# Attention with a mixture of soft experts: another opening, a reordered step between the two, and one weight piece issued sooner

## The chip, the cores and the metric

The kernel runs on one core of a Trainium2 chip. The metric is the device time of one execution in microseconds (us). TensorE (PE) multiplies matrices, VectorE (DVE) and ScalarE (ACT) work on vectors, GpSimd (POOL) fills buffers here, and SyncE (SP) issues all transfers between the chip's main memory and the core's buffers. Each engine runs its instructions in the order in which the program gives them; engines wait for each other through semaphores.

## What is computed

The reference has two stages. The first is attention in chunks: 4 batches, 8 heads, 768 positions, 64 values a head. Each chunk of 32 queries sees 8 memory keys and 56 keys around it.

```python
for c in range(nc):
    k_full = np.concatenate([mem_k, k_ctx], axis=2)
    v_full = np.concatenate([mem_v, v_ctx], axis=2)
    scores = scale * np.matmul(q_c, k_full.transpose(0, 1, 3, 2))
    a = np.exp(scores - np.max(scores, axis=-1, keepdims=True))
    a = a / (np.sum(a, axis=-1, keepdims=True) + 1e-09)
    out[:, :, c_start:c_end] = np.matmul(a, v_full)
```

Its result, as 3072 rows x of 512, goes into the second stage. Each of 32 slots takes a weighted mean of all rows (a softmax over the rows), eight experts of two layers work on four slots each, and every row takes a weighted mean of the slots' results (a softmax over the slots).

```python
logits = x @ phi
d = softmax(logits, over rows); slot_input = d.T @ x
for e in range(E):
    h = np.maximum(slot_input[e] @ w1[e], 0.0)
    slot_out[e] = h @ w2[e]
c = softmax(logits, over slots); out = c @ slot_out
```

All numbers are 32-bit floats. The two layers of weights are a bit over half of what the kernel reads.

## The kernel before, in words

**Units.** Attention goes over 24 tiles of 128 queries, two to a unit: units n = 0 to 11 (the loop in line 354). For a unit, `load_q`, `load_k` and `load_v` bring queries, keys and value rows into one of two slabs each (`kq_slab`, `v_slab`; unit n uses slab n % 2). Even and odd partitions of a slab hold the two heads of a pair; a transfer of keys or values fills one parity and one half, and the rest of the slab has to be zero. That zeroing is done once, in the opening (lines 150 to 161): VectorE and GpSimd share slab 0 of the keys and both slabs of the values, ScalarE does both halves of slab 1 of the keys, by copying zeros. Twelve dummy matmuls (`keep_warm(12)`) keep TensorE occupied until the keys are there.

**One unit on TensorE.** Transposes of the probabilities (`pt_ps`), the scores of the next unit (`s`), in every second unit the logits of the group before (`l`) or the dispatch of one (`D_ps`), transposes of the finished rows (`xt_ps`), and the values (`a`). VectorE does maxima, subtractions, sums and normalizing, ScalarE the exponentials and copies out of PSUM.

**Groups.** Four tiles of rows are a group G; there are six. For each, `logits` multiplies with phi, `dispatch_max` keeps a running maximum (`nmx`, in the tile `stats`) and copies the logits (`lT`), `dispatch_exp` takes the exponential, `dispatch_t` transposes it, `dispatch` multiplies it with the rows (`D_ps`), and `dispatch_sum` adds that to the running sum `D_sb`.

**The step between attention and experts** (lines 400 to 461). Groups 4 and 5 (NG - 2 and NG - 1) are still open here. TensorE transposes the last rows, dispatches group 4, takes the logits of group 5, brings the maximum of each slot to all partitions (`nmb`, `nm_ps`, `nms`, `b_ps`, `wrow`, `selw`), dispatches group 5, and makes the slots' input (`si_ps`, copied to `siT`), with which the experts begin (`h`). The normalizer of the slots (`wz`, `z_ps`, `rzd`) is made behind that. Groups of dummies stand between these.

**Experts and the end.** `expert_in` runs the first layer in four pairs of experts, `expert_out` the second layer, in two halves of the columns (`so`), and `combine` multiplies the combine weights with the slots' results and stores them (`o`).

**Weights and the transfer queue.** All transfers are issued by SyncE in program order, so one that waits holds back those behind it. The weights come in 32 pieces of 1 MB: 16 of w1, 16 of w2. Twelve slabs (`w_slab`, w_70 to w_81 in the order of instructions below) are theirs alone; eight more are the slabs of keys, values and rows once attention is done with them. `load_w(upto)` issues pieces up to a number: unit n asks for n + 2 pieces (line 398), from unit 9 on for as many as have a slab (`usable`). At unit n SyncE issues query and keys of unit n + 3, then value rows of unit n + 2, then that piece. A transfer also waits until the one eight places ahead of it in the queue has landed, because eight semaphores are used in turn.

```python
        if n + 2 < NUNIT:
            load_v(n + 2)
        load_w(usable[n] if n >= NUNIT - 3 else n + 2)
```

Of the kernel before, what the change touches and what calls it, by code (L numbers as in the profile page):

```python
# [10 lines left out]
F32 = mybir.dt.float32  # L11
F32R = mybir.dt.float32r
AF = mybir.ActivationFunctionType
ALU = mybir.AluOpType
AX = mybir.AxisListType

P = 128
# [7 lines left out]
NU = B * UPB  # L25
UU = 2
NUNIT = NU // UU
# [3 lines left out]
KB = NPAIR * KW  # L31
# [35 lines left out]
def tile_attn_softmoe(  # L67
# [44 lines left out]
    def load_v(n):  # L112
        t = v_slab[n % NIN]
        for par in range(2):
            sp.dma_start(t[par:P:2, par], vw[n, par])
# [28 lines left out]
    def keep_warm(n):  # L144
        if n:
            w_ps = ps.tile([P, P], F32, tag="T", name="fill_ps", bufs=2)
            for _ in range(n):
                pe.matmul(w_ps, lhsT=warm, rhs=warm, start=True, stop=True)

    dve.memset(warm, 0.0)  # L150
    dve.memset(kq_slab[0][:, 0:KB], 0.0)
    pool.memset(kq_slab[0][:, KB:2 * KB], 0.0)
    make_identity(nc, ident)
    for i in range(NIN):
        dve.memset(v_slab[i][:, 0], 0.0)
        pool.memset(v_slab[i][:, 1], 0.0)
    for par in range(2):
        act.copy(
            out=kq_slab[1][:, KB * par:KB * par + KB].rearrange("p (o n) -> p o n", n=104),
            in_=warm[:, 0:104].rearrange("p (o n) -> p o n", o=1).broadcast_to([P, KB // 104, 104]),  # L160
        )
    keep_warm(12)

    load_q(0)
    load_q(1)
# [1 line left out]
    load_k(1)  # L167
    load_v(0)
    sp.dma_start(phi_sb, phi.rearrange("(kc p) s -> p kc s", p=P))
    dve.tensor_reduce(out=sel, in_=ident.rearrange("p (g s) -> p s g", s=NSLOT), axis=AX.X, op=ALU.add)  # L170
    pool.tensor_copy(out=gsum, in_=sel.rearrange("p (o s) -> p o s", o=1).broadcast_to([P, 4, NSLOT]))

# [99 lines left out]
    def dispatch_max(G, l_ps):  # L272
        dve.tensor_reduce(out=nmx[G], in_=l_ps, axis=AX.X, op=ALU.max, negate=True)
        if G:
            dve.tensor_tensor(out=nmx[G], in0=nmx[G], in1=nmx[G - 1], op=ALU.min)
        lT[G] = wk.tile([P, P], F32, tag="lT", name=f"lT{G}")
        dve.tensor_copy(out=lT[G], in_=l_ps)

    def dispatch_exp(G, l_ps):
        d = wk.tile([P, P], F32, tag="d", name=f"d{G}", bufs=1)  # L280
        act.activation(out=d, in_=l_ps, func=AF.Exp, bias=nmx[G], scale=1.0, accum_out=zg[G])
        dexp[G] = d
        if G:
            act.activation(out=alpha[G], in_=nmx[G - 1], func=AF.Exp, bias=nmx[G], scale=-1.0)
# [32 lines left out]
        pe.transpose(t_ps, c[G].rearrange("p u s -> p (u s)"), ident)  # L317
        act.copy(out=cst[:, G, :], in_=t_ps)

    def dispatch(G):  # L320
        D_ps = ps.tile([P, DM], F32, tag="L", name=f"D_ps{G}")
        for g in range(4):
            pe.matmul(
                D_ps[32 * g:32 * g + 32, :],
                lhsT=dT[G][:, 32 * g:32 * g + 32],
                rhs=x_slab[G % 2][:, g, :],
                start=True, stop=True,
            )
        return D_ps

    def dispatch_z(G):
        if G:
            dve.scalar_tensor_tensor(out=zg[G], in0=zg[G - 1], scalar=alpha[G], in1=zg[G], op0=ALU.mult, op1=ALU.add)
# [14 lines left out]
    for u in range(UU):  # L348
        softmax(u, scores(u))
    load_kq(2)  # L350
    load_v(1)
    load_w(1)
    a_ps = {}
    for n in range(NUNIT):
        us = (2 * n, 2 * n + 1)
        last = n + 1 == NUNIT
        Gl = (n - 3) // 2 if n >= 3 and n % 2 == 1 else None
        Gd = (n - 4) // 2 if n >= 4 and n % 2 == 0 else None
        pts = [transpose_p(u) for u in us]
        if n >= 1:  # L360
            for u in us:
                normalize(u - 2, a_ps[u - 2])
        normalizer(n)
        if not last:
            s_ps = [scores(u + 2) for u in us]
        if n + 3 < NUNIT:
            load_kq(n + 3)
        if Gd is not None:
            dispatch_t(Gd)
        if Gl is not None:  # L370
            l_ps = logits(Gl)
        if n >= 1:
            transpose_x(us[0] - 2)
        if not last:
            for u, t in zip(us, s_ps):
                softmax(u + 2, t)
        if Gd is not None:
            combine_exp(Gd)
        if Gl is not None:
            dispatch_max(Gl, l_ps)  # L380
            dispatch_exp(Gl, l_ps)
            if Gl >= 1:
                combine_div(Gl - 1)
        a_ps[us[0]] = values(us[0], pts[0])
        if last:
            transpose_x(us[1] - 2)
            normalize(us[0], a_ps[us[0]])
            dispatch_t(NG - 2)
        a_ps[us[1]] = values(us[1], pts[1])
        if n >= 1 and not last:  # L390
            transpose_x(us[1] - 2)
        if Gd is not None:
            D_ps = dispatch(Gd)
            dispatch_z(Gd)
            dispatch_sum(Gd, D_ps)
        if n + 2 < NUNIT:
            load_v(n + 2)
        load_w(usable[n] if n >= NUNIT - 3 else n + 2)

    normalize(NU - 1, a_ps[NU - 1])  # L400
    transpose_x(NU - 2)
    D_ps = dispatch(NG - 2)
    load_w(usable[NUNIT])
    keep_warm(1)
    dispatch_z(NG - 2)
    dispatch_sum(NG - 2, D_ps)
    transpose_x(NU - 1, last=True)
    keep_warm(3)
    l_ps = logits(NG - 1)
    combine_in(NG - 2)  # L410
    dispatch_max(NG - 1, l_ps)
    dispatch_exp(NG - 1, l_ps)
    keep_warm(4)

    nm = nmx[NG - 1]
    nm_ps = ps.tile([NSLOT, 4, NSLOT], F32, tag="X", name="nm_ps")
    nmb = wk.tile([P, NSLOT], F32, tag="nmb", name="nmb", bufs=1)
    dve.tensor_copy(out=nmb, in_=nm.broadcast_to([P, NSLOT]))
    pe.transpose(nm_ps.rearrange("p g s -> p (g s)"), nmb, ident)
    nms = wk.tile([NSLOT, NSLOT], F32, tag="nms", name="nms", bufs=1)  # L420
    dve.tensor_reduce(out=nms, in_=nm_ps.rearrange("p g s -> p s g"), axis=AX.X, op=ALU.min)
    nms4 = wk.tile([NSLOT, 4, NSLOT], F32, tag="nms4", name="nms4", bufs=1)
    dve.tensor_copy(out=nms4, in_=nms.rearrange("p (o s) -> p o s", o=1).broadcast_to([NSLOT, 4, NSLOT]))
    dispatch_t(NG - 1)
    b_ps = ps.tile([P, 1], F32, tag="X", name="b_ps")
    pe.matmul(b_ps, lhsT=nms4.rearrange("p g s -> p (g s)"), rhs=ident[0:NSLOT, 0:1], start=True, stop=True)
    D_ps = dispatch(NG - 1)
# [4 lines left out]
    act.activation(out=wrow, in_=nm, func=AF.Exp, bias=nmt, scale=-1.0)  # L432
    selw = wk.tile([P, NSLOT], F32, tag="selw", name="selw", bufs=1)
    dve.tensor_scalar(out=selw, in0=sel, scalar1=wrow, scalar2=None, op0=ALU.mult)
    dispatch_sum(NG - 1, D_ps)
    combine_in(NG - 1)
    keep_warm(5)

    si_ps = ps.tile([P, NKC, NSLOT], F32, tag="X", name="si_ps")
    for kc in range(NKC):  # L440
        pe.matmul(si_ps[:, kc, :], lhsT=D_sb[:, kc, :], rhs=selw, start=True, stop=True)
    siT = wk.tile([P, NKC, NSLOT], F32, tag="siT", name="siT", bufs=1)
    dve.tensor_copy(out=siT, in_=si_ps)
    keep_warm(2)

    dispatch_z(NG - 1)
    wz = wk.tile([P, 1], F32, tag="wz", name="wz", bufs=1)
    dve.tensor_tensor(out=wz, in0=wrow, in1=zg[NG - 1], op=ALU.mult)
    z_ps = ps.tile([P, 1], F32, tag="L", name="z_ps")
    pe.matmul(z_ps, lhsT=gsum.rearrange("p g s -> p (g s)"), rhs=wz, start=True, stop=True)  # L450
    rzd = wk.tile([P, 1], F32, tag="rzd", name="rzd", bufs=1)
    dve.tensor_scalar_add(rzd, z_ps, 1e-9)
    dve.reciprocal(out=rzd, in_=rzd)
# [156 lines left out]
```

## Time and profile before

| | |
|---|---|
| time of three runs | 170.72, 170.78, 170.84 us; median 170.78 |
| the profiled execution | 170.87 us, its span 169.1 us |
| busy share of the span | PE 83%, PEld (weight loads) 61%, DVE 59%, ACT 36%, POOL 4% |
| main memory | 60.16 MB read, 6.29 MB written, 393 GB/s over the span |
| chain that ended last | PE 61%, transfers 19%, no cause shown ("issue") 7%, DVE 5% |

The profile is of one execution. Times count from the start of its span. The chain that ended last is followed back from the last instruction, at each step to what released it; its rows give start, length and what ran. The timeline gives start, length, engine, line, operation, output<-inputs and, in brackets, the idle time before it and what ended it. Nearly all lines are 61, that of a helper which records every operation, so groups are told apart by the names of the tiles. PE's rows are matmuls; each has a weight load beside it on PEld, and a matmul of 32-bit floats stands as two records (a transpose as one).

### The profile page before, as it was taken

The page shows a single profiled execution, that of the slowest core. Times are in us where ns is not written, and L with a number is a line of the kernel's source. Part 1 is how long each engine was busy: PE and PEld are TensorE (multiplying, and loading weights), DVE is VectorE, ACT ScalarE, POOL GpSimd, SP SyncE. Part 2 cuts the span into 40 slices and gives each one's busy share as a digit, 9 for nine tenths or more (in the row PEclk, how much of TensorE's full clock was granted, in tenths as well). Part 3 has the DMA queues.
Part 4 walks back from the last instruction along what each step waited for, and adds up shares of the span by engine and source line. Part 5 has one row for each costly group of instructions (what it writes and reads, how often), then busy time and mean ns, then how long its engine had stood idle before and what let it go on. Part 6 is the DMA issues. An engine that isn't in the chain of part 4 may idle for free.

```text
span 169.1 us, 6025 instructions
## 1 busy us (share of the span) xinstructions
PE 139.8 (83%) x2681; PEld 103.0 (61%) x2681; DVE 99.8 (59%) x216; ACT 61.7 (36%) x130; POOL 7.5 (4%) x12
## 2 busy tenths in 40 slices
PE   7648589869999699988879988999999999887800
PEld 7538478658768576866469756657555555453500
DVE  6579588785769993999499967445400101081620
ACT  8043343526462545364418445230222100071520
POOL 8400000000000000000000202000000000000000
PEclk9999999999999999999999999999999999999995
DMA  5999999999999999999995999999999999999896
GB/s 202 336 364 399 415 422 417 426 411 423 413 415 419 419 414 414 425 408 424 412 425 221 326 401 432 417 421 419 428 411 422 415 421 426 409 418 414 359 408 243
DMA packets 12457, 66.84 MB, mean 395 GB/s; under 512 B 2192, under 2 KB 2192, under 8 KB 6800
## 3 DMA queue, kind: packets, MB, share of 16 engines
q1 hardware_dynamic: 12432, 66.46, 96.8%
q8 instruction: 21, 0.34, 0.8%
q14 instruction: 4, 0.03, 0.0%
HBM read 60.16 MB, written 6.29 MB: 393 GB/s over the span
## 4 chain that ended last, share of the span: by engine, by line
PE 61%; DMA 19%; issue 7%; DVE 5%; ACT 2%; DVEq 0%; SPq 0%
DMA w<-in_w_dram 16%; PE a L61 15%; PE s L61 13%; PE xt_ps L61 8%; PE pt_ps L61 7%; PE l L61 4%; PE D_ps L61 4%; PE o L61 3%; DMA kq<-in_kT_dram 3%; PE so L61 2%; PE fill_ps L61 2%; PE dt_ps L61 2%; DVE kq L61 1%; DVE v L61 1%; DVE p L61 1%
## 5 line engine op out<-in xcount | busy, mean ns | idle before, releaser
L61 PE MATMUL a<-v,pt 128*32 128x128 f32 x768 | 25.7, 275 | 6.5 <-issue 6.5
L61 PEld LDWEIGHTS a<-v,pt 128*32 128x32 f32 x768 | 20.9, 110 | 9.8 <-issue 9.5
L61 PE MATMUL s<-kq 128*32 128x128 f32 x768 | 24.1, 274 | 2.9 <-DMA kq<-in_kT_dram 1.7
L61 ACT COPY xT<-xt_ps 128x512 f32<-128x512 f32 (+1 forms) x24 | 13.8, 577 | 29.6 <-PE xt_ps L61 29.6
L61 PEld LDWEIGHTS s<-kq 128*32 128x32 f32 x768 | 20.4, 110 | 5.4 <-issue 3.5
L61 ACT ACTIVATE p<-p 128x512 f32<-128x512 f32 x24 | 14.8, 630 | 13.3 <-DVE p L61 13.3
L61 DVE TENSOR_TENSOR x<-a,z 128x512 f32<-128x512 f32 x24 | 15.9, 685 | 6.3 <-PE a L61 6.3
L61 DVE TENSOR_TENSOR p<-s,mx 128x512 f32<-128x512 f32 x24 | 16.7, 696 | 0.8
L61 DVE TENSOR_REDUCE mx<-s 128x8 f32<-128x512 f32 x24 | 16.3, 678 | 1.4 <-PE s L61 1.1
L61 PE MATMUL xt_ps<-ident,x 128*128 128x128 f32 x96 | 15.6, 284 | 1.0 <-issue 1.0
L61 ACT COPY pt<-pt_ps 128x512 f32<-128x512 f32 x24 | 13.0, 589 | 7.1 <-PE pt_ps L61 7.1
L61 DVE TENSOR_REDUCE z<-p 128x16 f32<-128x1024 f32 x12 | 14.5, 1212 | 0.7 <-ACT p L61 0.7
L61 PE MATMUL pt_ps<-ident,p 128*128 128x128 f32 x96 | 13.0, 277 | 2.3 <-ACT p L61 2.3
L61 PEld LDWEIGHTS pt_ps<-ident,p 128*128 128x128 f32 x96 | 10.5, 141 | 6.4 <-ACT xT L61 3.4
L61 PEld LDWEIGHTS xt_ps<-ident,x 128*128 128x128 f32 x96 | 10.3, 140 | 4.9 <-issue 3.7
L61 PE MATMUL so<-w,hT 128*32 128x256 f32 x192 | 11.3, 381 | 0.6 <-DMA w<-in_w_dram 0.6
L61 PE MATMUL h<-w,siT 128*32 128x256 f32 x192 | 10.8, 380 | 0.0
L61 PE MATMUL fill_ps<-warm 128*128 128x128 f32 x54 | 9.0, 325 | 1.1 <-DVE warm L61 1.1
L61 PEld LDWEIGHTS fill_ps<-warm 128*128 128x128 f32 x54 | 8.3, 237 | 1.9 <-DVE warm L61 1.0
L61 PE MATMUL o<-sh,cst 32*128 32x256 f32 x96 | 8.0, 404 | 1.6 <-DVE v L61 0.6
L61 PEld LDWEIGHTS so<-w,hT 128*32 128x32 f32 x192 | 5.8, 110 | 5.6 <-DMA w<-in_w_dram 1.5
L61 DVE COPY hT<-ht_ps 128x32 f32<-128x32 f32 x8 | 1.2, 187 | 13.0 <-PE ht_ps L61 8.6
(94 smaller groups left out, 133.2 us busy)
## 6 DMA issues: line engine op xcount, KB each, us to landing
w<-in_w_dram SPq DMA_DIRECT2D x24, 1024.0 KB, 11.5
v<-in_vw_dram SPq DMA_DIRECT2D x24, 512.0 KB, 8.8
kq<-in_kT_dram SPq DMA_DIRECT2D x24, 312.0 KB, 9.4
kq<-in_qT_dram SPq DMA_DIRECT2D x12, 512.0 KB, 9.8
v<-in_w_dram SPq DMA_DIRECT2D x4, 1024.0 KB, 12.6
out_dram<-v SPq DMA_DIRECT2D x8, 512.0 KB, 5.0
kq<-in_w_dram SPq DMA_DIRECT2D x2, 1024.0 KB, 13.4
x<-in_w_dram SPq DMA_DIRECT2D x2, 1024.0 KB, 11.5
```

What stands on the lines that cost most here:

```text
L61: return self.tc.keep_in_program_order(f(*args, **kwargs))
```

## The change

It has three parts.

**Opening.** GpSimd zeroes the second half of key slab 1 as well, ScalarE only the first half. The twelve large dummies become four, and forty small ones of 32 columns in four strips follow. `load_v(1)`, the value rows of unit 1, is issued right behind phi, ahead of query and keys of unit 2.

**A weight piece.** In unit 8 (NUNIT - 4) two pieces are issued instead of one, so the eleventh slab (w_80) is filled ahead of the last unit's value rows.

**The step.** The last transposes and the logits of group 5 come ahead of the dispatch of group 4, which gets PSUM of another tag ("A" instead of "L"). The copy of the logits becomes a function of its own, `dispatch_lT`, and in the step it follows the broadcast of the maximum. The sum of group 4 on VectorE follows `nms4`. The normalizer's `dispatch_z`, `wz` and `z_ps` come ahead of the slots' input. Fifteen dummies in five places become seven.

```diff
-    pool.memset(kq_slab[0][:, KB:2 * KB], 0.0)
+    for i in range(NIN):
+        pool.memset(kq_slab[i][:, KB:2 * KB], 0.0)
...
-    for par in range(2):
-        act.copy(
-            out=kq_slab[1][:, KB * par:KB * par + KB].rearrange("p (o n) -> p o n", n=104),
-            in_=warm[:, 0:104].rearrange("p (o n) -> p o n", o=1).broadcast_to([P, KB // 104, 104]),
+    act.copy(
+        out=kq_slab[1][:, 0:KB].rearrange("p (o n) -> p o n", n=104),
+        in_=warm[:, 0:104].rearrange("p (o n) -> p o n", o=1).broadcast_to([P, KB // 104, 104]),
+    )
+    keep_warm(4)
+    fill_ps = ps.tile([P, NSLOT], F32, tag="T", name="fill_ps", bufs=2)
+    for i in range(40):
+        j = i % 4
+        pe.matmul(
+            fill_ps[32 * j:32 * j + 32, :], lhsT=warm[:, 0:NSLOT], rhs=warm[:, 0:NSLOT], start=True, stop=True
         )
-    keep_warm(12)
...
     sp.dma_start(phi_sb, phi.rearrange("(kc p) s -> p kc s", p=P))
+    load_v(1)
...
     load_kq(2)
-    load_v(1)
     load_w(1)
...
-        load_w(usable[n] if n >= NUNIT - 3 else n + 2)
+        load_w(usable[n] if n >= NUNIT - 3 else n + 2 + (n == NUNIT - 4))
...
     transpose_x(NU - 2)
-    D_ps = dispatch(NG - 2)
+    keep_warm(1)
+    transpose_x(NU - 1, last=True)
+    keep_warm(2)
+    dispatch_z(NG - 2)
+    l_ps = logits(NG - 1)
+    D_ps = dispatch(NG - 2, "A", 2)
     load_w(usable[NUNIT])
-    keep_warm(1)
-    dispatch_z(NG - 2)
-    dispatch_sum(NG - 2, D_ps)
-    transpose_x(NU - 1, last=True)
-    keep_warm(3)
-    l_ps = logits(NG - 1)
-    combine_in(NG - 2)
     dispatch_max(NG - 1, l_ps)
-    dispatch_exp(NG - 1, l_ps)
-    keep_warm(4)
...
+    dispatch_exp(NG - 1, l_ps)
+    dispatch_lT(NG - 1, l_ps)
+    keep_warm(1)
...
+    dispatch_sum(NG - 2, D_ps)
     dispatch_t(NG - 1)
+    combine_in(NG - 2)
...
+    dispatch_z(NG - 1)
+    wz = wk.tile([P, 1], F32, tag="wz", name="wz", bufs=1)
+    dve.tensor_tensor(out=wz, in0=wrow, in1=zg[NG - 1], op=ALU.mult)
     dispatch_sum(NG - 1, D_ps)
     combine_in(NG - 1)
-    keep_warm(5)
+    z_ps = ps.tile([P, 1], F32, tag="T", name="z_ps", bufs=2)
+    pe.matmul(z_ps, lhsT=gsum.rearrange("p g s -> p (g s)"), rhs=wz, start=True, stop=True)
+    keep_warm(2)
```

On SyncE, in the opening (v_67 is the slab of the value rows of unit 1, kq_64 that of queries and keys of units 0 and 2):

```order
 L61 DMA v_66<-in_vw_dram 64x2048 x2
 L61 DMA phi_sb<-in_phi_dram 128x4x32
+L61 DMA v_67<-in_vw_dram 64x2048 x2
 L61 DMA kq_64<-in_qT_dram 128x1024
 L61 DMA kq_64<-in_kT_dram 64x1248 x2
-L61 DMA v_67<-in_vw_dram 64x2048 x2
 L61 DMA w_70<-in_w_dram 128x2048
```

The value rows of unit 1 moved ahead of the query and keys of unit 2, which wait for the first scores.

On SyncE, from unit 8 to unit 9 (w_79 to w_81 are weight slabs, v_67 the slab of the value rows of unit 11):

```order
 L61 DMA v_66<-in_vw_dram 64x2048 x2
 L61 DMA w_79<-in_w_dram 128x2048
+L61 DMA w_80<-in_w_dram 128x2048
 L61 DMA v_67<-in_vw_dram 64x2048 x2
-L61 DMA w_80<-in_w_dram 128x2048
 L61 DMA w_81<-in_w_dram 128x2048
 L61 DMA kq_64<-in_w_dram 128x2048
```

One weight piece moved ahead of the value rows of unit 11, which wait for the values of unit 9.

On TensorE, in the step between attention and experts, before (behind the last logits):

```order
L61 MATMUL l_1769<-xT_1762,phi_sb 32x128
L61 MATMUL lt_ps_1786<-ident,lT_1679 128x128
L61 MATMUL fill_ps<-warm 128x128 x4
L61 MATMUL nm_ps<-ident,nmb 32x128
L61 MATMUL dt_ps_1808<-ident,d_1792 128x128
L61 MATMUL b_ps<-ident,nms_1806 128x1
L61 MATMUL D_ps_1814<-x_69,dT_1810 32x512 x4
L61 MATMUL lt_ps_1827<-ident,lT_1790 128x128
L61 MATMUL fill_ps<-warm 128x128 x5
L61 MATMUL si_ps<-selw,D_sb 128x32 x4
L61 MATMUL fill_ps<-warm 128x128 x2
L61 MATMUL z_ps<-wz,gsum 128x1
```

And in the changed kernel, from the same place on (D_ps_1811 is the dispatch of group 4, D_ps_1843 that of group 5):

```order
L61 MATMUL l_1794<-xT_1787,phi_sb 32x128
L61 MATMUL D_ps_1811<-x_68,dT_1749 32x512 x4
L61 MATMUL fill_ps<-warm 128x128
L61 MATMUL nm_ps<-ident,nmb 32x128
L61 MATMUL dt_ps_1835<-ident,d_1821 128x128
L61 MATMUL lt_ps_1839<-ident,lT_1712 128x128
L61 MATMUL b_ps<-ident,nms_1832 128x1
L61 MATMUL D_ps_1843<-x_69,dT_1837 32x512 x4
L61 MATMUL lt_ps_1859<-ident,lT_1824 128x128
L61 MATMUL z_ps<-wz,gsum 128x1
L61 MATMUL fill_ps<-warm 128x128 x2
L61 MATMUL si_ps<-selw,D_sb 128x32 x4
```

The dispatch of group 4 moved from ahead of the last transposes to behind the last logits, the product `z_ps` from behind the slots' input to ahead of it, and there are fewer dummies.

More of the change, by code (lines that the diff above doesn't have):

```diff
@@ L275, in dispatch_max, with dispatch_lT @@
             dve.tensor_tensor(out=nmx[G], in0=nmx[G], in1=nmx[G - 1], op=ALU.min)
+    def dispatch_lT(G, l_ps):
         lT[G] = wk.tile([P, P], F32, tag="lT", name=f"lT{G}")
@@ L318, in combine_t, with dispatch @@
         act.copy(out=cst[:, G, :], in_=t_ps)
-    def dispatch(G):
-        D_ps = ps.tile([P, DM], F32, tag="L", name=f"D_ps{G}")
+    def dispatch(G, tag="L", bufs=1):
+        D_ps = ps.tile([P, DM], F32, tag=tag, name=f"D_ps{G}", bufs=bufs)
         for g in range(4):
@@ L380, in tile_attn_softmoe @@
             dispatch_max(Gl, l_ps)
+            dispatch_lT(Gl, l_ps)
             dispatch_exp(Gl, l_ps)
@@ L397, in tile_attn_softmoe @@
             load_v(n + 2)
-        load_w(usable[n] if n >= NUNIT - 3 else n + 2)
+        load_w(usable[n] if n >= NUNIT - 3 else n + 2 + (n == NUNIT - 4))
     normalize(NU - 1, a_ps[NU - 1])
     transpose_x(NU - 2)
-    D_ps = dispatch(NG - 2)
-    load_w(usable[NUNIT])
-    keep_warm(1)
-    dispatch_z(NG - 2)
-    dispatch_sum(NG - 2, D_ps)
-    transpose_x(NU - 1, last=True)
-    keep_warm(3)
-    l_ps = logits(NG - 1)
-    combine_in(NG - 2)
+    keep_warm(1)
[4 more added lines that the diff above has]
+    D_ps = dispatch(NG - 2, "A", 2)
+    load_w(usable[NUNIT])
     dispatch_max(NG - 1, l_ps)
-    dispatch_exp(NG - 1, l_ps)
-    keep_warm(4)
     nm = nmx[NG - 1]
-    nm_ps = ps.tile([NSLOT, 4, NSLOT], F32, tag="X", name="nm_ps")
     nmb = wk.tile([P, NSLOT], F32, tag="nmb", name="nmb", bufs=1)
     dve.tensor_copy(out=nmb, in_=nm.broadcast_to([P, NSLOT]))
+    dispatch_exp(NG - 1, l_ps)
+    dispatch_lT(NG - 1, l_ps)
+    keep_warm(1)
+    nm_ps = ps.tile([NSLOT, 4, NSLOT], F32, tag="X", name="nm_ps")
     pe.transpose(nm_ps.rearrange("p g s -> p (g s)"), nmb, ident)
@@ L443, in tile_attn_softmoe @@
     dve.tensor_copy(out=siT, in_=si_ps)
[L444 to L450, printed above, removed]
+    keep_warm(1)
     rzd = wk.tile([P, 1], F32, tag="rzd", name="rzd", bufs=1)
```

## The prediction

> **What bounds the kernel now.** I read the page first: which engines are busy, and what queues there are besides the data.
>
> ```profile
> PE 139.8 (83%) x2681; PEld 103.0 (61%) x2681; DVE 99.8 (59%) x216; ACT 61.7 (36%) x130; POOL 7.5 (4%) x12
> ...
> q8 instruction: 21, 0.34, 0.8%
> ```
>
> PE works 83% of the span, and the transfers look busy all the time, so the question is which of the two ends last, and where. The second view is the transfers by stretch of the span (columns: from:to, length, busy time of each engine, granted clock, share of the DMA engines, GB/s).
>
> ```profile
> 2.00:6.00 4.00, 3.70 (x22) 3.51 (x20) 3.25 (x3) 2.38 (x3) 3.79 (x4) 1.00 0.97 368
> 6.00:14.00 8.00, 4.38 (x116) 3.76 (x120) 5.29 (x11) 2.32 (x4) 0.29 (x1) 1.00 0.99 343
> 14.00:89.00 75.00, 64.31 (x1492) 51.93 (x1488) 59.41 (x118) 32.55 (x69) 0.00 (x0) 1.00 1.02 418
> 89.00:97.00 8.00, 7.64 (x203) 6.68 (x199) 7.57 (x20) 5.37 (x14) 0.97 (x1) 1.00 0.73 265
> ```
>
> Between 14 and 89 us the stream runs at 418 GB/s without a break; this is its full rate here. It loses time twice. From 6 to 14 us it runs at 343: (418 - 343) x 8 us = 600 KB, or 1.4 us at 418. From 89 to 97 us it runs at 265: (418 - 265) x 8 = 1224 KB, or 2.9 us. (The first stretch, 368, loses 0.5 us more.) Everything behind such a hole lands later by what the hole cost, as long as the queue is not empty again.
>
> The third view, the timeline at the end, shows whether anybody waits for that.
>
> ```profile
> 145.99 1.07 PE L61 MATMUL so<-w,hT 128*32 128x256 f32 x16 [0.57 <-DMA w<-in_w_dram]
> ...
> 151.47 2.96 PE L61 MATMUL so<-w,hT 128*32 128x256 f32 x48
> ```
>
> At 145.99 PE has waited 0.57 us for a weight piece, and for nothing more: had the piece come sooner by more than 0.57, PE's own chain (attention, the step, the experts) would have been the bound. So two chains end within 0.6 us of each other. What the change is worth is the smaller of two gains: X, by which weight pieces land sooner, and 0.57 + Y, where Y is by how much sooner PE reaches its experts. Behind 145.99 come the combine, the last three pieces (x48) and the stores, each released by the one before, and all move with it.
>
> PE's own chain has a peculiarity in attention. In the chain that ended last (start, length, what) it stops for nothing that the profile names:
>
> ```profile
> 18.84 0.42 PE a L61 x5
> 19.26 1.02 PE pt_ps L61 x8
> 20.28 1.89 PE s L61 x64
> 22.17 0.59 PE xt_ps L61 x4
> 22.75 1.44 PE a L61 x44
> 24.19 0.51 issue
> ...
> 30.47 0.82 issue
> ```
>
> Between two of these stops stand 5 + 8 + 64 + 4 + 44 = 125 matmuls, with their loads 250 instructions. The page has 2681 + 2681 = 5362 of them and 21 transfers on an instruction queue: 255 for each. I read the stops as PE waiting for its next block of some 256 instructions, which shares the DMA engines with the data. Restarts lie at 18.84, 24.70 and 31.29: 5.86 and 6.59 us apart, 6.2 in the mean. A block whose work is shorter waits for the rest.
>
> The Trainium skill's page "Runtime: NRT & Kernel Launch", section "Instruction fetch mechanics", also speaks of refills of 256 instructions, but holds their cost to be mostly hidden. This trace does not agree: 0.51 and 0.82 us are on the chain. By that rule the added dummies could not hurt, and the last rival below would have no chance; the forecast would stay what it is.
>
> **The change part by part.** The opening, with the transfers as SyncE issues them and the zeroing that holds them up:
>
> ```profile
> 0.73 1.14 POOL L61 MEMSET kq<- 128x1248 f32 x1 [0.29 <-POOLq L598]
> ...
> 2.02 2.37 ACT L61 COPY kq<-warm 128x1248 f32<-128x1248 f32 x2
> 2.31 3.55 POOL L61 MEMSET v<- 128x2048 f32 x2
> ...
> 9.36 0.34 SPq L61 DMA_DIRECT2D kq<-in_qT_dram  x1
> ...
> 10.97 1.18 SPq L61 DMA_DIRECT2D v<-in_vw_dram  x2
> ```
>
> The key rows of unit 1 wait until ScalarE has zeroed both halves at 4.39. With one half on GpSimd (1.14 us, done near 3.0) and one on ScalarE (half of 2.37, done at 3.2) they are issued 0.9 us sooner, and on the same in-order queue the value rows behind them too. GpSimd's value zeroing slips by the same 1.14, from 5.86 to 7.0. Only the second transfer of value rows 1 needs its end, and it goes out at 10.97 or later today, so 7.0 holds up nothing; queued behind it is the query of unit 2 (9.36), which has 2 us left. Value rows 1 (1 MB) are issued near 7 instead of 11, so the queue is 2.5 us deeper just where it ran at 343 GB/s. I take the whole 1.4 us of the stretch from 6 to 14; the bounds are 0 (the low rate has another cause) and 1.9 (the first stretch is mended too). Query and keys of unit 2 now land behind 2.5 us more of data, less the 1.4: about 1 us later for PE's third pair of scores, at 20.28 today. The instruction gap there hides it; without that it would be 1 us of PE.
>
> The dummies: 44 instead of 12, each a double load and matmul (12 make 24 records):
>
> ```profile
> 1.00:5.80 4.80, 4.65 (x24) 4.46 (x24) 1.00 0.85 301
> ...
> 113.90:115.20 1.30, 1.16 (x10) 0.96 (x9) 1.00 1.03 422
> ```
>
> That puts 32 x 4 = 128 instructions, half a block, ahead of all of attention. Every block border now falls in the middle of what was a block. The number of borders and the time between them stay; which work stands between them does not. I take 0. Restarts differ by 0.7 us (5.86 to 6.59); from 18.84 to the last unit's values at 102.47 (row below) there are 83.6/6.2 = 13 borders, and thrown anew they give some 1.3 us either way (0.36 x the root of 13). The dummies themselves end before the first scores can start: 64 score records, in strips of 32 columns as the small dummies, took 1.89 us above, 30 ns each, or 50 at the slow rate of the opening (1.67 times, worked out below); 8 x 194 + 80 x 50 ns = 5.5 us from 1.05 on ends at 6.6. The keys hold the scores until 2.92 + 4.31 = 7.2 today, and nothing ahead of these keys changes:
>
> ```profile
> 2.92 4.31 DMA kq<-in_kT_dram
> ```
>
> The sooner weight piece. Today's rows near the hole, and the last unit's first values:
>
> ```profile
> 82.84 0.59 SPq L61 DMA_DIRECT2D w<-in_w_dram  x1
> 90.69 1.43 SPq L61 DMA_DIRECT2D v<-in_vw_dram  x2
> 92.17 1.06 SPq L61 DMA_DIRECT2D w<-in_w_dram  x2
> ...
> 102.47 1.01 PE a L61 x32
> ```
>
> Nothing is issued from 83.4 to 90.69, since the last value rows wait for PE to free their slab. A piece of 1 MB issued at 83.4 fills 2.5 of the 2.9 us. Its slab has never been used, so it waits only for the queue. The value rows behind it land up to 2.5 us later; they are needed at 102.47 and were issued 11.8 us before, so this stays hidden. X = 1.4 + 2.5 = 3.9 us; bounds 1.4 (the hole moves instead of closing) and 4.9.
>
> The step between attention and experts, chain first, then the timeline of what PE waits for in it:
>
> ```profile
> 106.83 1.00 PE D_ps L61 x8
> ...
> 109.35 1.01 PE l L61 x32
> ...
> 110.62 0.89 PE fill_ps L61 x8
> ...
> 113.94 1.12 PE fill_ps L61 x10
> 115.06 0.83 PE si_ps L61 x8
> 115.88 0.02 issue
> 115.91 0.29 DVE siT L61
> ...
> 117.02 1.04 PE h L61 x16
> ```
>
> ```profile
> 108.78 0.37 ACT L61 COPY xT<-xt_ps 128x256 f32<-128x256 f32 x1 [1.32 <-PE xt_ps L61]
> 109.18 0.42 DVE L61 COPY xT<-xt_ps 128x256 f32<-128x256 f32 x1 [0.53 <-ACT xT L61]
> ...
> 110.83 0.28 DVE L61 COPY lT<-l 128x128 f32<-128x128 f32 x1
> ...
> 113.75 0.75 DVE L61 SCALAR_TENSOR_TENSOR D_sb<-D_sb,stats,D_ps 128x512 f32<-128x512 f32 x1 [0.27 <-PE D_ps L61]
> ```
>
> First, the dispatch of group 4 (1.00) leaves its place ahead of the last transposes. Their copies move from 108.78 and 109.18 to 107.8 and 108.2; the second ends at 108.6, half of the logits (0.5) follow it, so they end at 109.1 instead of 110.36: 1.2 us. The dispatch then stands where 0.89 us of dummies stood, beside VectorE's maximum; the copy of the logits (0.28) stands behind the broadcast of the maximum, off the path. So PE keeps 1.2. Second, ten dummy records (1.12) after the last dispatch become four (0.45), with a transpose and the small product for the normalizer ahead of them; VectorE's last sum (0.75) ends within 0.1 us of that, so the slot inputs start 0.35 us sooner still. Third, from the end of the copy of the slot inputs (116.20) to the experts' first matmul (117.02) stands the normalizer's product with its two small VectorE steps, 0.8 us; it now runs before. VectorE's sum of group 4 (0.75, as in the row) falls between the minimum and the weights of the slots, where VectorE idles. Y = 1.2 + 0.35 + 0.8 = 2.35, say 2.4. Bounds: 1.6 (half of the first and third parts) and 2.9 (all dummies were in the way).
>
> The sum: the smaller of X = 3.9 and 0.57 + 2.4 = 3.0, so 3.0 us. The profiled execution took 170.87, with a span of 169.1 and 1.8 around it; 170.87 - 3.0 = 167.9. The median of the runs, 170.78, is 0.09 below it, within their own spread.
>
> **The rivals.**
>
> *The hole moves.* If the slowest DMA engine had no pause at 89 us, only the faster ones, then a sooner piece lets no last byte land sooner. For it: the share in that stretch is 0.73 and not near 0, so some engines worked. Against it: 1224 KB are missing. Then X = 1.4, and the time is 170.87 - 1.4 = 169.5.
>
> *PE starts cold.* Today's first 24 records take 4.65 us, 194 ns each; the ten at 113.9 take 116 ns. If small dummies don't bring PE to its rate, the first scores and what follows run at 194/116 = 1.67 times their time for about the 4 us that the dummies took: 1.6 us. Every later restart hangs on the first, so Y falls to 0.8: a gain of 1.4, and 169.5 again. Against it: 44 dummies keep PE occupied until about as late. The Trainium skill ("TensorE: Matmul & The Clock Gate", Part 1) has the warm-up go by some 3.4 us of activity and not by the number of matmuls, and gives 25 ns as the least distance of small ones; by that, 80 small records take at least 2 us, which speaks somewhat for this rival. No run here shows small dummies.
>
> *Nothing arrives sooner.* The low rate from 6 to 14 us has another cause and the hole moves too: X = 0, and PE still waits at 145.99 for the same piece. 170.8.
>
> *Instruction blocks come later* (the other side). With the holes filled, blocks share the DMA engines with more data, and with the borders moved they may stop PE for longer. If restarts lie 6.6 us apart (the longer of the two above) instead of 6.2, thirteen of them make PE 4.6 to 5.2 later, less Y + 0.57: 1.6 to 2.2 us slower, about 172.7. It decides from a mean of 6.2 + 3.0/13 = 6.43 on. Against it: from 14 to 89 us the stream is as full today as it can be.
>
> **How the numbers follow.** Forecast 0.64, the hole moves 0.14, cold start 0.10, nothing sooner 0.06, later blocks 0.06. A measurement of this kernel can tell about 0.2%, 0.34 us. All but the last two are faster: 0.88; the third rival is the same: 0.06; slower 0.06. The range: the forecast's own goes from 166.8 (X and 0.57 + Y both near 4, with 0.6 of luck at the borders) to 169.1 (Y = 1.6 and some bad luck); with the two rivals at 169.5 it reaches 169.7.
>
> **What would show it.** Over 340 GB/s, near 400, from 6 to 14 us; near 370 or more from 89 to 97. The experts' first matmul near 114.6. The wait for a weight piece near 143 small or gone. Stops named issue still every 125 or so matmuls, now inside other work, with a sum near today's. First scores as short as now (a cold start would stretch them). The forecast is wrong if the experts start before 115 and the end does not move, or if attention alone ends over 1 us later.

## The result, and the profile after

| | before | changed |
|---|---|---|
| median of the runs that were made together | 171.35 us (11 runs, 170.47 to 171.82) | 169.92 us (11 runs, 168.84 to 172.48) |
| ratio of the times | | 0.9925, 95% interval 0.9898 to 0.9952 |
| the profiled execution | 170.87 us, span 169.1 us | 170.30 us, span 168.5 us |

By the ratio the change is worth 0.75%, 1.28 us. The forecast was 3.0 us and a range up to 169.7: the direction is right, the size is less than half. The two profiled executions lie 0.57 us apart, so their rows explain that much directly; the rest of the 1.28 us is seen only in the times. The profiled executions of three experiments (x3, x8, x11) took over 1.5% longer than the fastest run of the same kernel, so only the times of these three are used.

The transfers by stretch in the changed kernel (columns as above), and under it the one stretch of the kernel before that the prediction did not show:

```profile
6.00:14.00 8.00, 4.84 (x78) 4.05 (x82) 4.61 (x8) 1.85 (x4) 1.18 (x2) 0.96 1.00 378
14.00:89.00 75.00, 67.33 (x1548) 54.39 (x1544) 59.17 (x120) 33.34 (x71) 0.00 (x0) 0.98 1.02 413
89.00:97.00 8.00, 5.88 (x125) 4.67 (x115) 7.17 (x18) 3.70 (x10) 0.97 (x1) 1.00 0.93 349
97.00:140.00 43.00, 41.12 (x672) 26.27 (x675) 15.74 (x56) 11.75 (x30) 0.98 (x1) 1.00 1.00 414
```

```profile
97.00:140.00 43.00, 40.82 (x629) 26.00 (x622) 14.76 (x53) 10.63 (x28) 0.98 (x1) 1.00 1.01 419
```

Both low stretches went up, 343 to 378 and 265 to 349 GB/s, so the pieces did go out into them. But neither reached full rate, and behind the hole the stream is now a little slower than before (414 against 419). What is left of it stands at the end of the weights. The chain that ended last, in the changed kernel and before:

```profile
88.22 1.87 PE a L61 x61
90.09 1.76 issue
91.85 0.41 PE a L61 x3
...
125.23 20.04 DMA w<-in_w_dram
145.31 1.07 PE so L61 x16
```

```profile
87.39 0.98 issue
...
88.75 1.88 PE a L61 x64
...
126.13 19.82 DMA w<-in_w_dram
```

The piece that PE waits for landed at 145.27 instead of 145.95 (start and length of its row, added): X came to 0.7 us instead of 3.9. PE still waits for it (timeline, idle time in brackets):

```profile
145.31 1.07 PE L61 MATMUL so<-w,hT 128*32 128x256 f32 x16 [0.48 <-DMA w<-in_w_dram]
```

PE was there at 144.83; before it was there at 145.42. So 0.57 + Y became 0.57 + 0.59. Y was 0.6 instead of 2.4, and the rows of PE say where it went: the last values, and the experts' first matmul, before and after.

```profile
105.17 1.08 PE L61 MATMUL a<-v,pt 128*32 128x128 f32 x32
116.95 4.31 PE L61 MATMUL h<-w,siT 128*32 128x256 f32 x76
```

```profile
106.37 1.08 PE L61 MATMUL a<-v,pt 128*32 128x128 f32 x32
116.36 4.96 PE L61 MATMUL h<-w,siT 128*32 128x256 f32 x88
```

The step shrank from 11.78 to 9.99 us, a gain of 1.79. But attention ended 1.20 later, and 1.79 - 1.20 = 0.59. Attention had been taken to be untouched.

### The profile page after: what moved, and what is told of

Its sections match the earlier page's. It is cut to its first block, busy times and chain, and to the rows that moved or that the text cites. A ratio compares the mean times of both kernels' runs of the same rounds, so it can differ in the third digit from the quotient of the medians.

```text
span 168.5 us, 6123 instructions
## 1 busy us (share of the span) xinstructions
PE 139.9 (83%) x2729; PEld 102.1 (61%) x2729; DVE 99.5 (59%) x216; ACT 60.4 (36%) x129; POOL 8.5 (5%) x13
## 4 chain that ended last, share of the span: by engine, by line
PE 55%; DMA 22%; DVE 7%; issue 6%; POOL 3%; ACT 2%; DVEq 0%; ACTq 0%; POOLq 0%
PE s L61 13%; DMA w<-in_w_dram 12%; PE a L61 10%; PE xt_ps L61 6%; DMA kq<-in_kT_dram 6%; PE h L61 5%; PE pt_ps L61 4%; DMA kq<-in_qT_dram 4%; PE o L61 3%; PE D_ps L61 3%; PE l L61 3%; PE so L61 2%; POOL v L61 2%; PE dt_ps L61 2%; DVE v L61 1%
## 5 line engine op out<-in xcount | busy, mean ns | idle before, releaser
L61 PE MATMUL s<-kq 128*32 128x128 f32 x768 | 27.8, 294 | 6.7 <-issue 3.0
L61 PE MATMUL a<-v,pt 128*32 128x128 f32 x768 | 25.0, 274 | 4.9 <-issue 4.9
L61 PEld LDWEIGHTS s<-kq 128*32 128x32 f32 x768 | 23.1, 119 | 8.3 <-issue 4.9
L61 PEld LDWEIGHTS h<-w,siT 128*32 128x32 f32 x192 | 6.0, 110 | 4.2 <-DVE siT L61 0.3
L61 PEld LDWEIGHTS o<-sh,cst 32*128 32x128 f32 x96 | 5.3, 184 | 4.3 <-DVE kq L61 1.4
## 6 DMA issues: line engine op xcount, KB each, us to landing
kq<-in_w_dram SPq DMA_DIRECT2D x2, 1024.0 KB, 10.1
```

Source lines behind the costliest of these rows:

```text
L61: return self.tc.keep_in_program_order(f(*args, **kwargs))
```

## The experiments

**Undoing one part.** First the sooner piece alone was taken back (in the changed kernel):

```diff
-        load_w(usable[n] if n >= NUNIT - 3 else n + 2 + (n == NUNIT - 4))
+        load_w(usable[n] if n >= NUNIT - 3 else n + 2)
```

> The changed kernel without the sooner weight piece, all else as changed. If the hole at 89 us was worth its 1.6 us on the slowest engine (last byte of the twelfth piece 1.6 us sooner in the changed kernel than before), the wait for a weight piece near 145 us grows to 1.5 us or more, the rate from 89 to 97 us falls back to near 265 GB/s, and the time is 1 to 1.6 us above the changed kernel's, no faster than the kernel before. If the hole only moved between engines, the time stays within 0.4 us of the changed kernel's.

Measured: 171.87 us, ratio to the kernel before 1.0021 (0.9988 to 1.0054). Without the piece nothing is left of the gain.

Then the step alone was put back into the old order, dummies included:

```diff
     transpose_x(NU - 2)
+    D_ps = dispatch(NG - 2)
...
-    D_ps = dispatch(NG - 2, "A", 2)
...
-    dispatch_sum(NG - 2, D_ps)
     dispatch_t(NG - 1)
```

> The changed kernel with the step between attention and experts as it was. The step took 9.9 us from the last unit's second values to the experts in the changed kernel and 11.8 before, so the experts start 1.9 us later here. If TensorE's own chain is one of two that end together, the time is 1 to 1.5 us above the changed kernel's and the wait for a weight piece near 145 us is gone. If weight pieces alone bound the end (slowest DMA engine), only what exceeds the present wait of 0.47 us is seen, and the sum is again about 1.4 us; both give that, unless the step's gain was never on the chain: then within 0.4 us.

Measured: 170.81 us, ratio 1.0017 (0.9981 to 1.0054). Again nothing is left. The profile shows the other side of the same balance: PE enters the second layer without a wait, the 32 matmuls in one row, while the piece had landed at 144.6 (issued 126.2, 18.4 to landing).

```profile
144.78 1.93 PE L61 MATMUL so<-w,hT 128*32 128x256 f32 x32
```

**One part alone.** The kernel before with only the piece, and with only the step:

```diff
-        load_w(usable[n] if n >= NUNIT - 3 else n + 2)
+        load_w(usable[n] if n >= NUNIT - 3 else n + 2 + (n == NUNIT - 4))
```

> The kernel before with the one sooner weight piece and nothing else. 'Two chains': the landings come some 1.6 us sooner, but PE's own chain had only 0.57 us to give, so the gain is 0.4 to 0.7 us (ratio 0.996 to 0.9975), and PE no longer waits for a piece at the first block of the second layer that waited. Rival 'the parts add' (each part takes its own time off, whatever the others do; undoing the piece cost 0.96%): gain 1.6 us, ratio 0.990.

Measured: 171.42 us, ratio 1.0009 (0.9976 to 1.0041). The rival, that the parts add, is out, but the 0.57 us that PE had to give did not come either. The chain shows why, and the transfers by stretch (the kernel before first) show what became of X:

```profile
92.82 1.54 PE s L61 x49
94.36 0.95 issue
95.31 0.64 PE s L61 x15
```

```profile
107.00:111.00 4.00, 4.00 (x58) 2.92 (x51) 1.84 (x7) 0.83 (x2) 0.00 (x0) 1.00 1.01 426
119.00:123.00 4.00, 4.00 (x80) 2.39 (x76) 1.19 (x6) 0.69 (x1) 0.00 (x0) 1.00 1.01 420
```

```profile
89.00:97.00 8.00, 6.59 (x147) 5.36 (x147) 7.43 (x19) 4.00 (x10) 0.97 (x1) 1.00 0.98 386
107.00:111.00 4.00, 4.00 (x58) 2.67 (x54) 1.68 (x4) 1.21 (x3) 0.00 (x0) 1.00 0.90 336
119.00:123.00 4.00, 4.00 (x81) 2.37 (x77) 2.76 (x13) 1.23 (x3) 0.00 (x0) 1.00 0.84 291
```

With the instructions at the same places as before, PE now stops 0.95 us after 49 of 64 score records, in the middle of the hole that the piece filled; the kernel before runs these 64 without a stop (its rows stand with the useless data below); its last values start at 106.87. And the stream, which is ahead by the piece, runs out of work twice: near 109 it waits for the slabs of the last values, near 121 for the slabs of the first experts, both freed by PE. The hole moved in part, to places where PE sets the pace.

> The kernel before with the reordered step and nothing else. 'Two chains': the experts begin 1.8 us sooner, near 115.2, and PE then waits 2.4 us instead of 0.57 for the same weight piece near 146, so the gain is 0 to 0.2 us (ratio 0.999 to 1.001). Rival 'the parts add' (undoing the step cost 0.92%): gain 1.6 us, ratio 0.991.

```diff
+    transpose_x(NU - 1, last=True)
...
     l_ps = logits(NG - 1)
+    D_ps = dispatch(NG - 2, "A", 2)
...
+    dispatch_z(NG - 1)
```

Measured: 171.68 us, ratio 1.0005 (0.9968 to 1.0041), as two chains expect: a sooner PE would wait for the same piece. That wait is not shown here, only the time is used.

**The hole filled with useless data.** To see whether it is the data that stops PE, the kernel before got one transfer more, of 1 MB that nobody uses; no weight piece comes sooner by it.

```diff
         load_w(usable[n] if n >= NUNIT - 3 else n + 2)
+        if n == NUNIT - 4:
+            sp.dma_start(w_slab[NW - 1].rearrange("p (k f) -> p k f", k=2), w1[0].rearrange("(p kc) f -> p kc f", kc=NKC)[:, 0:2, :])
```

> The kernel before with one transfer more: in unit 8, behind its weight piece, 1 MB that nobody uses is read into the slab of the twelfth piece, which gets its own data later as ever. The hole is filled, but no weight piece comes sooner. Theory 'coupled' (PE's instruction blocks come later when the hole is full of data): TensorE gets a new stop of about 0.95 us near 95 and goes from unit 10 to unit 11 in 9.0 us instead of 7.8, the last values start 1.2 to 1.7 us later than 105.2, the experts near 118.4, and the time is 0.6 to 1.1 us longer than before (ratio 1.003 to 1.007). Rival 'data costs nothing' (the later attention of the kernels with the sooner piece has another cause): the last values near 105.2 and ratio 0.999 to 1.001.

Measured: 172.64 us against 171.17, ratio 1.0091 (1.0058 to 1.0124). PE's rows (chain, then timeline):

```profile
92.09 1.88 PE s L61 x64
93.97 0.38 PE dt_ps L61 x2
```

```profile
93.07 1.54 PE s L61 x49
94.61 0.95 issue
95.56 0.64 PE s L61 x15
```

```profile
146.86 1.96 PE L61 MATMUL so<-w,hT 128*32 128x256 f32 x32
```

```profile
89.00:97.00 8.00, 6.34 (x145) 5.11 (x145) 7.45 (x19) 4.00 (x10) 0.97 (x1) 1.00 0.98 392
```

The first pair is the kernel before, the other rows the kernel with the useless data. The same 64 score records, which ran in one row before, are cut after 49 by the 0.95 us that the sooner piece brought too; from the first to the last of them it takes 3.13 us instead of 1.88. The last values start at 107.67, 2.5 us late: 1.25 in these scores, 0.27 at a longer stop at 102.96 (0.79 instead of 0.52), and 1.0 that was there at 92 already, which is scatter between executions as far as these runs tell. At the end PE waits for no piece (the 32 records at 146.86 in one row), so it is not weights, held up behind the useless data, that made it longer. So filling the hole has a price, paid by PE: the kernel got 0.9% slower, where 0.3 to 0.7% was expected; the interval begins at 0.58%. Before, PE ran over this place without a stop, after a queue that from 89 to 93 us moved 254 and 172 GB/s (two stretches of 2 us); with the useless data it moved 426 and 377. That the stop is the fetch of a block is still an inference from its place, every 256 instructions; that it comes with the data in the queue is shown.

The Trainium skill ("Runtime: NRT & Kernel Launch", section "Instruction fetch mechanics") takes the crossing of such a block to be mostly hidden. This pair of runs agrees where the queue ran low (no stop) and differs where it was full (0.95 us).

**Two sooner pieces.** The rest of the hole was filled as well:

```diff
-        load_w(usable[n] if n >= NUNIT - 3 else n + 2 + (n == NUNIT - 4))
+        load_w(usable[n] if n >= NUNIT - 3 else n + 2 + 2 * (n == NUNIT - 4))
```

> The changed kernel with two sooner pieces in unit 8 instead of one. Theory 'coupled': the rest of the hole was made by TensorE's own lateness, the stream then waits later for slabs that TensorE must free (near 109 and 121 us), so nothing more is gained: within 0.3% of the changed kernel, ratio 0.990 to 0.996 to the kernel before; the value rows of the last unit land 2.5 us later, and its values start no sooner than 106.3. Rival 'mean rate' (every gap of the queue that is closed lets the pieces land sooner by as much): the stretch from 89 to 97 us goes from 349 to over 400 GB/s, the pieces land 1.0 to 1.2 us sooner still, and as the changed kernel waits 0.5 us for a piece, it gets 0.4 to 0.6 us faster, ratio 0.989 or less.

Measured: 169.91 us, ratio 0.9927 (0.9896 to 0.9959), the changed kernel's own. Its transfers by stretch, and PE's wait:

```profile
89.00:97.00 8.00, 5.61 (x117) 4.38 (x108) 6.92 (x17) 3.38 (x10) 0.97 (x1) 1.00 1.01 416
97.00:107.00 10.00, 9.00 (x185) 6.51 (x188) 6.83 (x19) 5.63 (x14) 0.98 (x1) 1.00 1.01 419
107.00:111.00 4.00, 4.00 (x70) 2.89 (x60) 1.69 (x5) 0.96 (x2) 0.00 (x0) 1.00 0.89 328
```

```profile
145.01 1.07 PE L61 MATMUL so<-w,hT 128*32 128x256 f32 x16 [0.24 <-DMA w<-in_w_dram]
```

The hole is gone, 416 GB/s through it, and what was won shows up as a new dip at 107 to 111 us: (419 - 328) x 4 us = 364 KB, 0.9 us. The piece that PE waits for landed at 144.97, only 0.3 us sooner than in the changed kernel. The mean rate of a stretch is not the landing of what follows, as long as the stream waits for PE later on.

**The opening.** All of the old opening with the new piece and step; then only the old zeroing and the old place of the value rows, with the new dummies:

```diff
-    keep_warm(4)
-    fill_ps = ps.tile([P, NSLOT], F32, tag="T", name="fill_ps", bufs=2)
-    for i in range(40):
...
+    keep_warm(12)
...
-    load_v(1)
...
     load_kq(2)
+    load_v(1)
```

> The sooner piece and the reordered step as changed, the whole opening as before. Theory 'two chains' (the end is set by the later of PE's chain and the weights' landings; the piece gives the landings some 1.6 us, the opening gives them next to nothing): attention on PE ends as before (last values near 105.2), the step takes 10.0 us, so the experts begin near 115.2; the pieces land near 144.3; the time is 169.6 to 170.0 us, ratio 0.989 to 0.992, not slower than the whole change. Theory 'mean rate' (each term of the forecast's X holds, the opening's share of the landings with it): the first weight piece lands 1.4 us later than with the new opening, and the gain of the whole change (0.75%) shrinks to 0.2% or less, 170.9 or more.

Measured: 170.74 us, ratio 0.9975 (0.9938 to 1.0012). The time is nearer to what 'mean rate' expected, half a per cent above the changed kernel, with intervals that overlap. But its reason is not there: the first weight piece landed at 21.4, not 1.4 us later than in the changed kernel (22.2). Nor did attention end near 105.2, as 'two chains' had it: the last values start at 106.52, and the 0.95 us stop of x7 and x9 is back, at 94.0.

```diff
-    for i in range(NIN):
-        pool.memset(kq_slab[i][:, KB:2 * KB], 0.0)
+    pool.memset(kq_slab[0][:, KB:2 * KB], 0.0)
...
-    load_v(1)
...
     load_kq(2)
+    load_v(1)
```

> The changed kernel with the old zeroing (ScalarE does both halves of key slab 1) and the value rows of unit 1 in their old place; the new dummies stay. Theory 'two chains' with an opening whose transfers gain nothing: within 0.3% of the changed kernel, ratio 0.990 to 0.995 to the kernel before, and the first weight piece lands within 0.4 us of 22.2. Theory 'mean rate': the stretch from 6 to 14 us falls back to 343 GB/s, the landings of all weight pieces come 1.4 us later, and the ratio is 1.000.

Measured: 172.31 us, ratio 1.0044 (1.0010 to 1.0077). By the ratios that is 1.2%, 2.0 us, slower than the changed kernel, and slower than before, which neither theory had; the first weight piece landed at 24.1, 1.9 us later than in the changed kernel. The first scores of the changed kernel, and those and SyncE's transfers of this one:

```profile
7.29 3.21 PE L61 MATMUL s<-kq 128*32 128x128 f32 x64 [2.94 <-POOL gsum L61]
```

```profile
7.14 3.64 PE L61 MATMUL s<-kq 128*32 128x128 f32 x64 [2.79 <-POOL gsum L61]
```

```profile
6.85 0.59 SPq L61 DMA_DIRECT2D phi_sb<-in_phi_dram  x1
10.83 0.34 SPq L61 DMA_DIRECT2D kq<-in_qT_dram  x1
```

```profile
6.00:14.00 8.00, 5.76 (x72) 4.64 (x72) 4.73 (x8) 1.73 (x3) 0.29 (x1) 1.00 0.89 300
```

With the small dummies PE starts cold: 3.21 and 3.64 us for 64 score records that took 1.95 before. The query of unit 2 waits for those scores, so SyncE issues nothing from 7.4 to 10.83, and the rate falls to 300 GB/s. In the changed kernel the value rows of unit 1 stand in that gap. The loss shows in attention: the scores that wait for keys start at 34.74 instead of 33.56, the last values at 108.09 instead of 106.37, and at the end PE waits for no piece. So the new dummies and the sooner value rows belong together: one makes a gap that the other fills.

**Other dummies.** Four kernels with all else as changed. Each dummy record is two instructions, so a large dummy and a small one put in 4 each: 12 large are the borders of before, 32 more small ones move them by 128, 16 by 64; 8 large and 52 small by 192. In x1, x2 and x12 the first 64 score records take 1.95 or 1.96 us, so these start at the full rate. But in x2 and x12 the second 64 are slow all the same (3.07 and 3.43 us against 1.95 in x1); x11's are not compared.

```diff
-    keep_warm(4)
+    keep_warm(12)
...
-    for i in range(40):
+    for i in range(32):
```

> The changed kernel with its opening dummies undone: twelve large ones again instead of four large and forty small. Cold start (TensorE idles 3 us before the first scores and runs them, and the next pair, at about half rate): the first 64 score records take 1.95 us instead of 3.21, attention ends 1.2 us or more sooner, and the time falls 1 to 1.5 us below the changed kernel's, to some 2.5 us below the kernel before. Instruction-block borders (the 128 added instructions moved them into worse places): also faster, by about 1 us, because the borders go back as well; the next run separates the two. Slowest DMA engine (weight pieces bound the end whatever TensorE does): the first scores are short again, the experts start sooner, and the time stays within 0.4 us of the changed kernel's, with a longer wait for a weight piece.

> The changed kernel with twelve large and 32 small dummies: as many instructions as the changed kernel's opening plus none (176 in both), so the instruction-block borders stay where the change put them, but TensorE is kept busy until about 6 us. Cold start: as fast as the run with twelve large dummies alone, 1 to 1.5 us below the changed kernel. Block borders: as slow as the changed kernel, with a stop of 1.5 us or more near 90 us in the values of unit 9 and the experts starting 1 us later than with large dummies alone. Slowest DMA engine: within 0.4 us of the changed kernel.

> The changed kernel with 12 large and 16 small dummies in the opening: TensorE starts warm, and all borders of instruction blocks stand 64 instructions further than with 12 large dummies alone (128 further in the changed kernel and with 12 large and 32 small). Theory 'borders' (the place of the borders alone sets the sum of TensorE's stops in attention, 11.4 us at 0 and 7.9 us at 128, and the time follows it): a sum between 8 and 11 us and a time between 169.5 and 170.5 us, in the same order as the sum. Rival 'borders cost nothing' (restarts come in a fixed rhythm whatever stands between them): the last values start at the same time as at 0 and at 128 within 0.3 us, and the time is 169.3 to 170.6 with no order.

> The changed kernel with 8 large and 52 small dummies: borders 192 instructions further than with 12 large alone, TensorE kept occupied until about 6.2 us. Theory 'borders': again a sum of stops of its own, between 8 and 11.5 us, and the time in the order of the sums of the four places (0, 64, 128, 192): under 170 us if the sum is under 9, over 170 if it is over 10. Rival 'borders cost nothing': as for 64. Should the small dummies at the end leave TensorE cold, the first 64 score records take 3 us instead of 1.95, and the run counts for neither.

| | moved by | ratio (95% interval) | PE stops without a cause, 12 to 105 us |
|---|---|---|---|
| x1: 12 large | 0 | 0.9961 (0.9937 to 0.9984) | 11.7 us |
| x11: 12 large, 16 small | 64 | 0.9895 (0.9859 to 0.9930) | not compared |
| x2: 12 large, 32 small | 128 | 0.9906 (0.9869 to 0.9943) | 7.8 us |
| x12: 8 large, 52 small | 192 | 0.9914 (0.9886 to 0.9943) | 9.5 us |
| changed: 4 large, 40 small | 128 | 0.9925 (0.9898 to 0.9952) | 7.9 us |

The stops are the rows of the waits that name no releaser; a wait of 0.8 to 1.6 us before 12 us, ahead of the first transposes, which the kernels with moved borders have, is left out. For the kernel before, x1 and x2 (columns: who, waited for, us in total, times, longest):

```profile
PE a L61 <- issue: 6.5, 5, 2.4
PE l L61 <- issue: 1.8, 2, 1.3
...
PE s L61 <- issue: 1.2, 2, 0.8
PE xt_ps L61 <- issue: 1.0, 1, 1.0
```

```profile
PE a L61 <- issue: 7.5, 5, 1.8
PE s L61 <- issue: 2.5, 4, 0.9
PE l L61 <- issue: 1.5, 2, 1.2
...
PE xt_ps L61 <- issue: 0.2, 1, 0.2
```

```profile
PE a L61 <- issue: 4.2, 4, 1.8
PE s L61 <- issue: 3.6, 4, 1.3
```

Borders at the places of before go with the most stops, in all kernels whose profiles are used: 10.3 to 12.7 us (before, x1, x5, x7, x9) against 7.8 to 8.8 at 128 (changed, x2, x4, x6, x10). They also go with the most time; x11's interval lies clear of x1's, those of x2 and x12 just touch it, and among the three moved places the intervals don't tell an order. x1 and x2 differ in 32 small dummies and nothing else; the medians are 170.56 and 169.48. But the small dummies and the moved borders always come together here, and of the 3.9 us fewer stops in x2 only 0.6 reaches the last values (105.64 against 106.27). So that the borders make the time is not shown.

What had been expected of these runs did not come. For x1 two of the three theories had a kernel that is faster than the changed one by about 1 us; it came out slower by 0.4%, with intervals that overlap, and of the third only the longer wait for a piece came (1.03 us). x2 was to be 1 to 1.5 us faster than the changed kernel (cold start), or as slow, with a stop of 1.5 us or more near 90 us and its experts 1 us later than x1's (borders). It is 0.2% faster, which these runs can't tell from nothing; the stop came (1.76), but its experts start 0.6 us sooner than x1's. x12 fell between the bounds that it had been given. Since x2's second scores are slow too, no kernel with these borders ran all its scores at the full rate, so what the slow start costs in time is not measured. The versions x2 and x11 are the fastest measured, but not told apart from the change.

## Why the prediction was off

**The rule held.** The gain was the smaller of X and 0.57 + Y: 0.7 and 1.16 in the profiled execution, with a wait of 0.48 left. X was the smaller, so X set the time; but with X right, the measured Y alone would have held the gain to 1.16. Taking back either the piece or the step lost all of it (1.0021, 1.0017), and either alone brought nothing (1.0009, 1.0005).

**The step that failed: X = 1.4 + 2.5 = 3.9 us, with Y worked out as if PE didn't notice.** Its terms, one by one:

- *The hole, 2.5 us.* The prediction left the last value rows at 90.69, with the piece in front. They go out at 92.29, because PE frees their slab later: the stop of 1.76 us at 90.09 stands inside the values of unit 9, which have to be done first. So the hole is filled at one end and grows at the other; (349 - 265) x 8 us = 672 KB, 1.6 us. The twelfth piece confirms it, landing at 101.7 (issued 93.45, 8.2 to landing) instead of 103.3 (92.79, 10.5).
- *Given back later.* Of these 1.6 us, 0.7 is left at 145.27. (419 - 414) x 43 us = 215 KB, 0.5 us, accounts for a bit over half of what was given back. In x7 and x10 the giving back is seen whole, as dips at 107 and 119 us.
- *The opening, 1.4 us.* The stretch went from 343 to 378, not to 418, which is 280 KB or 0.7 us. The first weight piece landed 10.1 us after its issue in both, at 22.2 instead of 22.3, so of that nothing reached it in this execution: the value rows come sooner, the query of unit 2 and all behind it don't.

**Y = 2.4 was 0.6.** The step's first and third parts were right: the logits came 1.19 us sooner behind the last values (1.2 forecast), and from the slots' input to the experts 0.67 less (0.8). Of the second, 0.35, 0.2 came. But the first part had let the dispatch of group 4 stand beside VectorE's maximum for nothing, and that cost 0.28. The timeline of the changed kernel, and under it that of before:

```profile
110.36 1.02 PE L61 MATMUL D_ps<-x,dT 128*32 128x512 f32 x5
111.31 0.49 PE L61 MATMUL fill_ps<-warm 128*128 128x128 f32 x2
111.63 0.27 PE L61 MATMUL nm_ps<-ident,nmb 128*32 128x128 f32 x1
```

```profile
111.35 0.27 PE L61 MATMUL nm_ps<-ident,nmb 128*32 128x128 f32 x1
```

The dispatch of group 4 and one dummy stand longer than the dummies that they replace, and hold the broadcast of the maximum back by 0.28, from where it runs through to the slots' input; behind the last dispatch 0.2 comes back. 1.19 - 0.28 + 0.2 + 0.67 is the measured 1.8.

The rest of Y went in attention, 1.20 us; the prediction had named an end of attention over 1 us later as a sign of being wrong. At the values of unit 9 PE was still 0.53 ahead (88.22 against 88.75). From there to the last values it lost 1.73: 1.76 in the stop inside these values and 0.49 more between the last unit's two groups of values (3.26 against 2.77), less the 0.52 at 100.73 that only the kernel before stops. That data in the hole stop PE is shown at the old borders (x9). At the new ones it is argued: every kernel with them whose profile is used has the piece, and stops there for 1.76 us with one sooner piece (changed, x2, x4, x6) and 2.03 with two (x10).

**The rivals.** *Instruction blocks come later* had 0.06, priced at all thirteen borders (4.6 to 5.2 us); its mechanism is what happened, at one border and for about 1 us, and x9 shows it by itself, at another border than the changed kernel's. "From 14 to 89 us the stream is as full today as it can be" was right and missed the point: the hole was where it was not. *The hole moves* was nearest as to X (1.4), but for another reason than it gave: the twelfth piece did land 1.6 us sooner, and it was the slabs that PE frees that took this back.

*PE starts cold* came true: the first 64 score records took 3.21 us instead of 1.95, the second 3.38. The argument against it failed in its size. The prediction let the 80 small records last 4 us, to 6.6; all dummies were done at 4.35, and PE was idle for 2.94 us:

```profile
1.05 3.30 PE L61 MATMUL fill_ps<-warm 128*128 128x128 f32 x88 [1.05 <-DVE warm L61]
```

It was priced by what PE loses, 1.6 us. The two pairs lost 2.7, but about as much went into stops that disappeared, the 2.37 us at 16.47 above all. What is left of its price are the transfers behind the first scores, up to 2.0 us in x6, and the value rows cover that here. The Trainium skill ("TensorE: Matmul & The Clock Gate", Part 1) puts the return to the slow rate behind some 3.4 us without work. Here PE was idle for 2.94 us before the slow scores, and small dummies are not needed for it: x7 has the twelve large ones, waits 1.32 us for its first scores, and runs the second 64 slowly:

```profile
13.20 3.04 PE L61 MATMUL s<-kq 128*32 128x128 f32 x64
```

What makes these scores slow stays open.

**The borders, taken as 0 with 1.3 either way.** The stops came to 7.9 us instead of 10.5, 2.6 less, about what the slow scores cost (1.26 and 1.43). Whether the borders or the later start of PE made them fewer is not told apart.

**What stays open.** The rows explain 0.57 of the 1.28 us. The profiled executions of the changed kernel and of x5 (old opening) end alike, at 170.30 and 170.31, though their medians are 169.92 and 170.74. Where the opening's half per cent lies in time is not seen in them. The opening alone was not run.

## What to carry to other kernels

A gap in the transfer queue is not free time to be filled: look who else is stopped by it (here TensorE, it seems for its own instructions), and who ended it (here TensorE freeing a slab), before its bytes are counted as a gain. Where two chains end within a microsecond of each other and each holds slabs that the other needs, a gain on one is the smaller of the two only after the later places where they meet; work out those first. Edits that each undo a side effect of another (small dummies and sooner value rows; sooner piece and shorter step) have to be judged together, because each alone measures as nothing or worse.

## What the runs showed of the hardware

- Data in the transfer queue stopped TensorE, at a place that recurs every 256 instructions: no stop in the kernel before, where the queue moved 254 and 172 GB/s ahead of it, and 0.95 us at the same instruction in x9 (426 and 377 GB/s) and x7 (422 and 385).
- Small dummies in the opening, which also move all block borders by 64 to 192 instructions, came with 0.5 to 0.7% less time (0.9961 against 0.9895 to 0.9914).
- 80 matmul records of 32 columns in four strips were done 3.30 us after the start of the dummies, with eight large records ahead of them; the prediction had given them all 5.5 us.
- 64 score records took 3.21 us after 2.94 us of idle TensorE, while the granted clock of the stretch from 6 to 14 us reads 0.96. The column shows the slow rate in some executions only: in x4 it reads 0.50 from 8 to 14 us (first scores 3.10), in x6 and x10 1.00 (3.64 in both).
